# Output products as Strassen's seven half-size products in an attention and gated FFN kernel, with three attention banks, a ring of features and a row sum on GpSimd

## The chip, the cores and the metric

The kernel runs on one core of a Trainium2 chip. The metric is the device time in microseconds (us) of one execution. The kernel before took 346.88 us (median of three runs, 346.76 to 348.04). In later sessions its medians lay between 347.5 and 350.3 us, so each experiment is compared with runs of the kernel before that were made beside it on the same chip.

## The reference

```python
B, H, S, D = 8, 8, 576, 64                    # q, k, v: [B, H, S, D] float32, drawn as 0.1 * randn
k_p = k.reshape(B, H, S // 8, 8, D).mean(3)   # keys and values pooled by 8: 72 rows a head
v_p = v.reshape(B, H, S // 8, 8, D).mean(3)
attn = softmax(q @ k_p.T / sqrt(D)) @ v_p     # per head
x = attn.transpose(0, 2, 1, 3).reshape(4608, 512)
out = (relu(x @ w_gate) * (x @ w_val)) @ w_out     # 512 -> 1536 -> 512, float32
```

## The kernel before

The 4608 tokens go through the FFN in nine chunks of 512 tokens. While chunk c is in its gate and value products, TensorE also makes the output products of chunk c-1 and the attention of batch c+1. This is "the stage of chunk c". The attention of a stage is a list of small pieces of work, one after each unit of large matmuls.

```python
def scores(b, h):                      # one head: two banks, one exponential
    ps = ps_at.tile([P, 2, 512], F32)              # ps_at: 2 tiles of 2 banks
    for j, c0, i0, cnt in (...): nc.tensor.matmul(out=ps[:SP, j, ...], ...)
    nc.scalar.activation(out=e[:SP], in_=ps[:SP, :, :HS], func=AF.Exp, ...)
...
def values(b, t):                      # weights times pooled v -> px (piece_pool: 4 buffers)
...
def back(b, t, eng):                   # px -> x_T, most by a DMA transpose that SyncE issues
    eng.dma_start_transpose(out=dst, in_=x)
...
def q_dma(b):                          # q -> qT, one large DMA transpose, same queue
    nc.sync.dma_start_transpose(out=qT_tiles[b], in_=q16_tiles[b]...)
...
def prep(b, load_next):                # all on GpSimd, in this order
    for i in range(KJ // 2): run(pool_k(b, i, nc.gpsimd))
    if load_next: load_k(b + 1); load_q(b + 1); load_v(b + 1)      # 576 KB each
    for g in range(NG): run(pool_v(b, g, nc.gpsimd))
...
for c in range(1, n_chunks):
    units = weave_units(gv[:-1], outs)             # outs: 4 x (12 matmuls of 512 columns)
    if c + 2 < B: q_dma(c + 2); prep(c + 2, c + 3 < B)
    if c + 1 < B: others = attention(c + 1)        # [kt], [], four pairs of heads, values ...
    for i, unit in enumerate(units): unit(); run(others[i])
```

GpSimd's queue is in order. In the kernel before nothing in it waits for the FFN, so it runs ahead. SyncE's queue holds the transposes and the stores of finished blocks of 128 rows, also in order.

The softmax here doesn't subtract the row's maximum and nothing guards it: scores larger than these inputs give would overflow.

## Time and profile before

| what (one profiled run) | value |
|---|---|
| span | 346.0 us, TensorE busy for 96% |
| stage of chunk 1 | 30.48 us |
| stage of chunk 2 | 36.30 us, 1.15 of it waiting for features |
| stages of chunks 3 to 6 | 35.00 us each, TensorE full |
| stage of chunk 7, without attention | 31.08 us |
| from the stage of chunk 8 to the end | 46.53 us |

A stage is cut where each chunk's first gate matmul starts. Its length is what the time is made of, since TensorE hardly waits.

These are lines of the timeline of SyncE's queue in the kernel before (start us, length us, engine, line, operation, count). The length of a row is how long SyncE was held by the instructions that issue the transfers. It is not the time until the data landed, and a row of several instructions includes the gaps between them:

```profile
112.18 8.51 SPq L324 DMA_TRANSPOSE x_T<-px  x3
...
126.23 0.60 SPq L366 DMA_DIRECT2D out_dram<-fout  x1
126.94 7.27 SPq L218 DMA_TRANSPOSE qT<-q  x1
...
148.21 8.54 SPq L324 DMA_TRANSPOSE x_T<-px  x3
...
163.26 4.47 SPq L218 DMA_TRANSPOSE qT<-q  x1
```

"The time of a transpose" below is this time of SyncE; where a landing or the packets themselves were read, the text says so. A piece of features held SyncE for 3.88, 1.22 and 1.21 us in the first of these rows and for 1.45, 1.19 and 1.19 us in the row at 148.21; the rest of a row of three is mostly waiting for the next piece. The queries of a batch take 4.5 to 7.3 us, and a single store stands ahead of them.

### The profile page before, as it was taken

What the parts mean: (1) busy time and instruction counts of PE and PEld (TensorE: products, weight loads), DVE (VectorE), ACT (ScalarE), POOL (GpSimd) and SP (SyncE); (2) the same over time, 40 slices, a digit from 0 to 9 for tenths busy, and PEclk for the clock granted to TensorE, in tenths of its full rate; (3) what the DMA queues carried; (4) which work ended last, traced back from release to release, by engine and by line L of the source; (5) the groups of instructions that cost most, each with busy time, mean ns of one, the idle gap of its engine ahead of it and who ended that gap; (6) DMA issues with size and microseconds to landing.
All of it is one profiled execution on the core that took longest, in us unless ns stands there. A gap on an engine that the chain in (4) does not pass through costs nothing.

```text
span 346.0 us, 5538 instructions
## 1 busy us (share of the span) xinstructions
PE 333.7 (96%) x2140; PEld 179.3 (52%) x2140; DVE 158.7 (46%) x291; ACT 129.4 (37%) x232; POOL 132.4 (38%) x184
## 2 busy tenths in 40 slices
PE   7799999999999989999999999999999999999995
PEld 2578895455454435544545455445544444444443
DVE  7446636435624434353435343534253322398840
ACT  1344472374263225423442345234523232322221
POOL 8447509999999898307910710000000000000000
PEclk9979999999999999999999999999999999999999
DMA  7999996998996799962414351421134111211113
GB/s 114 196 205 199 167 213 116 197 167 161 142 175 112 132 165 154 190 112 60 94 40 48 78 97 34 75 53 32 30 70 52 40 32 34 57 28 35 30 58 95
DMA packets 48762, 35.36 MB, mean 102 GB/s; under 512 B 29600, under 2 KB 42144, under 8 KB 48736
## 3 DMA queue, kind: packets, MB, share of 16 engines
q0 software_dynamic: 16496, 18.88, 33.4%
q1 hardware_dynamic: 32096, 16.00, 25.0%
q8 instruction: 17, 0.28, 0.4%
q10 hardware_dynamic: 144, 0.13, 0.1%
q14 instruction: 9, 0.07, 0.1%
HBM read 37.75 MB, written 9.44 MB: 136 GB/s over the span
## 4 chain that ended last, share of the span: by engine, by line
PE 87%; DMA 6%; DVE 4%; issue 1%; POOL 1%; ACT 1%; DVEq 0%; ACTq 0%; POOLq 0%
PE mm_ps L343 51%; PE mm_ps L388 24%; PE at_ps L232 4%; DMA x_T<-px 4%; PE at_ps L302 3%; DMA v_in<-in_v_dram 2%; DVE h L359 2%; PE mm_ps L328 1%; PE mm_ps L253 1%; PE mm_ps L411 1%; PE mm_ps L178 1%; PE mm_ps L281 0%; PE mm_ps L208 0%; POOL k_in L116 0%; DVE px L312 0%
## 5 line engine op out<-in xcount | busy, mean ns | idle before, releaser
L359 DVE TENSOR_TENSOR h<-mm_ps,relu 128x512 f16<-128x512 f32 (+1 forms) x120 | 97.1, 819 | 150.3 <-PE mm_ps L343 140.1
L343 PE MATMUL mm_ps<-x_T,wg_sb 128*128 128x512 f16 (+1 forms) x480 | 113.7, 359 | 2.3 <-DMA x_T<-px 1.1
L343 PE MATMUL mm_ps<-x_T,wv_sb 128*128 128x512 f16 (+1 forms) x480 | 113.4, 359 | 0.4 <-DVE kpT1u L191 0.4
L349 ACT ACTIVATE relu<-mm_ps 128x512 f16<-128x512 f32 (+1 forms) x120 | 66.4, 553 | 118.9 <-PE mm_ps L343 115.2
L388 PE MATMUL mm_ps<-wo_sb,h 128*128 128x512 f16 x420 | 101.5, 379 | 0.4 <-DVE h L359 0.2
L343 PEld LDWEIGHTS <-wv_sb 128*128 128x128 f16 x480 | 47.1, 98 | 47.3 <-DVE kpT1u L191 0.7
L343 PEld LDWEIGHTS <-wg_sb 128*128 128x128 f16 x480 | 45.0, 99 | 38.8 <-DMA x_T<-px 1.6
L388 PEld LDWEIGHTS <-h 128*128 128x128 f16 x420 | 40.0, 98 | 45.6 <-DVE h L359 0.7
L237 ACT ACTIVATE expT<-at_ps 72x576 f16<-72x576 f32 x56 | 33.6, 642 | 19.8 <-PE at_ps L232 19.8
L397 ACT COPY fout<-mm_ps 128x512 f32<-128x512 f32 x31 | 18.1, 585 | 46.4 <-PE mm_ps L388 46.4
L145 POOL TENSOR_TENSOR tree_b<-tree_a 72x256 f32<-72x256 f32 (+1 forms) x45 | 32.5, 721 | 3.5
L312 DVE TENSOR_TENSOR px<-at_ps,prd 128x256 f16<-128x256 f32 (+1 forms) x80 | 30.2, 418 | 1.4
L139 POOL TENSOR_TENSOR tree_a<-k_in 96x512 f32<-96x512 f16 x21 | 24.1, 1149 | 15.5 <-DMA k_in<-in_k_dram 15.5
L139 POOL TENSOR_TENSOR tree_a<-v_in 72x512 f32<-72x512 f16 x24 | 27.6, 1152 | 0.1
L150 POOL TENSOR_TENSOR stat<-tree_b 72x128 f16<-72x128 f32 x24 | 10.8, 451 | 37.4 <-PE at_ps L302 35.7
L302 PEld LDWEIGHTS <-expT 72*128 72x128 f16 (+1 forms) x280 | 12.9, 100 | 8.8 <-issue 3.0
L302 PE MATMUL at_ps<-stat,expT 72*128 72x65 f16 (+1 forms) x280 | 14.7, 194 | 0.4 <-DVE stat L265 0.4
L309 DVE RECIPROCAL prd<-at_ps 128x8 f32<-128x8 f32 (+1 forms) x40 | 8.0, 201 | 13.8 <-PE at_ps L302 13.8
L330 ACT COPY x_T<-mm_ps 128x512 f16<-128x512 f16 (+1 forms) x10 | 5.6, 564 | 14.1 <-PE mm_ps L328 14.0
L150 POOL TENSOR_TENSOR kp<-tree_b 96x128 f16<-96x128 f32 x21 | 9.5, 452 | 1.6
L172 PE MATMUL mm_ps<-warm_sb 128*128 128x512 f16 x24 | 8.6, 491 | 1.2 <-DVE warm_sb L483 1.2
L232 PE MATMUL at_ps<-qT,kpT1u 128*72 128x32 f16 x64 | 9.3, 229 | 0.0
(61 smaller groups left out, 157.8 us busy)
## 6 DMA issues: line engine op xcount, KB each, us to landing
out_dram<-fout SPq DMA_DIRECT2D x31, 256.0 KB
k_in<-in_k_dram POOLq DMA_DIRECT2D x7, 576.0 KB, 7.3
q<-in_q_dram POOLq DMA_DIRECT2D x7, 576.0 KB, 9.8
v_in<-in_v_dram POOLq DMA_DIRECT2D x7, 576.0 KB, 15.1
wg_sb<-in_moe_w_gate_dram POOLq DMA_DIRECT2D x6, 256.0 KB, 11.2
wv_sb<-in_moe_w_val_dram POOLq DMA_DIRECT2D x6, 256.0 KB, 11.0
wo_sb<-in_moe_w_out_dram POOLq DMA_DIRECT2D x3, 512.0 KB, 10.3
out_dram<-fout SPq DMA_DIRECT2D x16, 64.0 KB
```

Source lines behind the costliest of these rows:

```text
L139: eng.tensor_tensor(out=cell["a"][:n], in0=src[:, :, :4 * D], in1=src[:, :, 4 * D:], op=ALU.add)
L145: eng.tensor_tensor(out=cell["c"][:n], in0=a[:n, :, :2 * D], in1=a[:n, :, 2 * D:], op=ALU.add)
L150: eng.tensor_tensor(out=out_ap, in0=c[:n, :, :D], in1=c[:n, :, D:], op=ALU.add)
L232: nc.tensor.matmul(out=ps[:SP, j, c0:c0 + cnt * QP], lhsT=kpTs[b % 2][j][:, h, :], rhs=queries(b, h, i0, cnt), start=True, stop=True,)
L237: nc.scalar.activation(out=e[:SP], in_=ps[:SP, :, :HS], func=AF.Exp, scale=EXP_SCALE)
L302: nc.tensor.matmul(out=ps[:n, half, c0:c0 + D + 1], lhsT=weights(b, h, t), rhs=stats[b % 2][:SP, g, s0:s0 + D + 1], start=True, stop=True,)
L312: nc.vector.tensor_tensor(out=x[:n, half * NG // 2:(half + 1) * NG // 2, :, :], in0=xs, in1=rd[:n, half].unsqueeze(3).to_broadcast([n, NG ...
L343: nc.tensor.matmul(out=t[:, :n], lhsT=w[:, ci, fsl], rhs=x_T[:, ci, p0:p0 + n], start=(ci == 0), stop=(ci == n_co - 1),)
L349: nc.scalar.activation(out=relu[:, :n], in_=ps[0][:, :n], func=AF.Relu)
L359: nc.vector.tensor_tensor(out=h, in0=val, in1=relu, op=ALU.mult)
L388: nc.tensor.matmul(out=t, lhsT=h_tiles[c, fo][:, ts * P:(ts + 1) * P], rhs=wo_sb[:, fo, :], start=(fo == 0), stop=(fo == n_fo - 1),)
L397: nc.scalar.copy(o, t)
```

## The change

The intent is to save arithmetic. The output product of a chunk (512 x 1536 by 1536 x 512) is cut into halves in all three directions, and Strassen's scheme needs seven half-size products in place of eight. VectorE makes the sums of h in float16 and the sums of results in float32. The rest of the change makes room for this and rearranges the start: one accumulator bank is taken from the attention, features are kept for four batches only (a ring), and k and v of batches 0 and 1 are loaded in wider rows. The core of the diff:

```diff
-    ps_at = ... bufs=2 (tiles of two banks)
+    ps_at = ... bufs=3 (tiles of one bank)
+    ps_acc = ... bufs=1
-    x_T = const_pool.tile([P, n_co, NTOK], F16, name="x_T")
+    RING = 4 * S
+    x_T = const_pool.tile([P, n_co, RING], F16, name="x_T")
-    fout_pool ... bufs=3
+    fout_pool ... bufs=2
@@ scores @@
-        nc.scalar.activation(out=e[:SP], in_=ps[:SP, :, :HS], func=AF.Exp, scale=EXP_SCALE)
+        for j, parts in ...:                       # one bank and one exponential a half
+            ps = ps_at.tile([P, 512], F32, name="at_ps", tag="at_ps")
+            ...
+            nc.scalar.activation(out=e[:SP, j, :], in_=ps[:SP, :HS], func=AF.Exp, ...)
@@ out_products, new @@
+        def pr1(): nc.scalar.copy(p1, product(a, e, True))
+        def pr2(): nc.scalar.copy(rows[0][:, :, :HD], product(b, g, False))
+        ...
+        def pr5():
+            nc.scalar.copy(p5, product(S[0], T[0], True))
+            plus(rows[1][:, :, HD:], u3, p5, nc.gpsimd)     # the only FFN work on GpSimd
+            send(1)                                         # two blocks of rows at once
+        def pr3():
+            plus(rows[0][:, :, HD:], product(S[3], h, False), u2)
+            send(0)
@@ attention @@
+        soon = 3 if b == 3 else 1                  # values of batch 3 in three units in a row
@@ main @@
+        weight_sums(nc.vector)                     # before stage 1: four sums of w_out's quarters
... (wide loads, pooling by selection matmuls, permuted h cut to 128 columns: left out)
```

## The prediction

> **What bounds the kernel now.** I read the head of the page first, then the chain that ended last, then a table of one row per chunk's stage (cut where each chunk's first gate matmul starts), and last the timeline inside a stage.
>
> ```profile
> PE 333.7 (96%) x2140; PEld 179.3 (52%) x2140; DVE 158.7 (46%) x291; ACT 129.4 (37%) x232; POOL 132.4 (38%) x184
> ...
> PE 87%; DMA 6%; DVE 4%; issue 1%; POOL 1%; ACT 1%; DVEq 0%; ACTq 0%; POOLq 0%
> ```
>
> TensorE (PE) is busy for 96% of the span and makes up 87% of the chain; no other engine reaches half. The chain also gives the price of a matmul where nothing waits (start us, length us, what):
>
> ```profile
> 276.36 3.45 PE mm_ps L343 x16
> ...
> 339.23 2.63 PE mm_ps L411 x24
> ```
>
> Sixteen 512-column matmuls in 3.45 us are 0.216 us each; twenty-four 256-column ones in 2.63 us are 0.110 us each, although each has its own weight load. Half-width products therefore cost nearly half.
>
> The stages of chunks 1 to 8 (columns: window and its length, then busy us and count of PE, weight loads, DVE, ACT, POOL; clock; DMA share; GB/s):
>
> ```profile
> 61.68:92.16 30.48, 30.48 (x203) 16.01 (x203) 14.74 (x30) 13.49 (x23) 28.59 (x40) 1.00 0.96 165
> 92.16:128.46 36.30, 35.15 (x216) 17.61 (x215) 15.02 (x30) 13.92 (x24) 33.09 (x44) 1.00 0.89 145
> 128.46:163.46 35.00, 35.00 (x215) 17.68 (x216) 13.63 (x28) 13.92 (x24) 16.83 (x23) 1.00 0.77 133
> 163.46:198.45 34.99, 34.99 (x216) 17.68 (x215) 14.33 (x29) 13.91 (x24) 15.85 (x22) 1.00 0.38 65
> ...
> 268.43:299.51 31.08, 31.08 (x145) 14.11 (x144) 8.30 (x12) 9.50 (x16) 0.00 (x0) 1.00 0.15 36
> 299.51:333.66 34.15, 33.78 (x157) 15.05 (x155) 29.53 (x13) 9.51 (x16) 0.00 (x0) 1.00 0.14 34
> ```
>
> Stage 7, which has no attention, is 144 matmuls x 0.216 = 31.1 us: nothing but its arithmetic. An attention stage adds 3.7 us of small matmuls and is again full: 35.0 of 35.0. So what a stage loses or gains in PE time or in PE waits goes straight into the span. Only stage 2 waits, 36.30 against 35.15: the chain has 12.26 us of the DMA that writes the features of batch 3 there, and PE waited for it at 127 us. Stage 8 waits a little, with DVE nearly full (29.53), because its twelve permuted products h take 2.4 us each.
>
> **What the Trainium skill says.** (1) "TensorE: Matmul & The Clock Gate", section "Back-to-back issue gap", gives N / 2.4 + 2.5 ns for a warm matmul, 216 ns at 512 and 109 ns at 256; the trace agrees (0.216 and 0.110). (2) "PSUM — Partial Sum Buffer", section "Specifications (TRN2)": eight banks of 512 float32 per partition. Before, four single-bank product tiles plus two two-bank attention tiles fill them; after, it is four, three single-bank attention tiles and one accumulator. (3) "VectorE: DVE Perf Modes", section "The perf-mode tier table": a tensor_tensor with 16-bit operands in SBUF runs at two elements a cycle, with a PSUM operand at one. No such all-16-bit operation is in this trace; the PSUM ones agree with one: 0.69 us for 512 elements and 0.42 for 256, so 1.04 ns an element and some 0.16 us fixed. (4) "SBUF — State Buffer", section "Who interferes with whom": a DVE instruction with two SBUF inputs and a GpSimd one that reads SBUF exclude each other for a whole instruction. The trace has no such meeting yet. The h products, with one SBUF input, took 0.69 us with GpSimd busy (71 us) and idle (300 us), which does not contradict it.
>
> **Gains, part by part.**
> Strassen: per chunk 48 x 0.216 = 10.37 us become 7 products x 12 matmuls x 0.110 = 9.24 us. That is 1.13 us, and for seven chunks 7.9 us, all on the path.
> Batch 3's values move to three units in a row in stage 2, so their features are sent earlier: the 1.3 us (36.30 - 35.00) goes.
> Start and chunk 0: pooling v on PE takes 10 matmuls in place of 16 for each of two batches, 12 x 0.11 = 1.3 us; the waits of 0.42 and 0.46 us just before stage 1 go, since the last feature copies move behind the next chunk's products; the key turns become 18 small matmuls in place of 7, about 0.3 us worse. Together 1.9 us. That v itself lands sooner than its 13 us I do not expect: it is the same bytes with shorter runs.
> Last stage: only 128 of 512 columns are still permuted, so h falls from 2.4 us to about 1.2 and PE's waits of 0.4 us vanish; I take 0.5 us.
> Sum of the gains: 11.6 us.
>
> **Losses, part by part.** The order of instructions of the changed kernel shows in every pair of heads that the fourth score tile waits for ACT: four one-bank tiles go through three banks. This is how the pair runs today:
>
> ```profile
> 68.45 0.29 PE L232 MATMUL at_ps<-qT,kpT0l 128*72 128x288 f16 x1
> ...
> 68.84 0.31 PE L232 MATMUL at_ps<-qT,kpT0u 128*72 128x32 f16 x2
> ...
> 68.92 1.18 ACT L237 ACTIVATE expT<-at_ps 72x576 f16<-72x576 f32 x2 [1.83 <-PE at_ps L232]
> 68.99 1.03 PE L343 MATMUL mm_ps<-x_T,wg_sb 128*128 128x512 f16 x4
> ```
>
> PE is through in 0.54 us and ACT works behind it. After, with the pair's start as zero: the first tile's data are there at 0.29, its exponential (288 of 576 columns; 0.64 us less 288 x 0.84 ns, the slope between 512 columns at 0.59 and 576 at 0.64, so 0.40) ends at 0.72, and with some 0.06 us for the semaphore the fourth tile starts at 0.78 where it would start at 0.39. That is 0.39 us of idle PE a pair. The pair that directly follows the second product is worse: ACT first copies that product (0.585 us), so its first exponential ends near 1.1 and the wait is 0.77 us. Stage 1: 4 x 0.39 = 1.6 us. Stages 2 to 6: 3 x 0.39 + 0.77 = 1.94 us each, 9.7 us. Together 11.3 us: more than Strassen gives.
>
> Weight sums: four DVE operations of 1536 elements stand before the first h of stage 1. At two elements a cycle 0.16 + 768 x 1.04 ns = 0.96 us each, 3.8 us. They start about 1.5 us after PE begins that stage's first products, and PE runs on until the key transposes need the bank that first h frees: by my count it stops for 2.4 us, and for up to 5 if GpSimd, busy there with v, holds the shared port.
>
> Sums of h: eight of 768 elements a chunk, 0.16 + 384 x 1.04 ns = 0.56 us each, 4.5 us on a DVE that has 20 us free in a stage. They lie beside PE, except that the key copies (2 x 0.75) stand behind the first two sums and the first pair needs them. If GpSimd is at work then, a sum waits up to 1.15 us, and the first pair loses up to 1 us; that can be so in stages 2 to 5, since the sum of rows on GpSimd now holds back the pooling behind it. 0 to 4 us, I take 2.
> Chunk 4 wraps round the ring: 256-column halves, 12 x 16 x 0.110 against 12 x 8 x 0.216, 0.4 us.
> Sum of the losses: 14.1 us without contention, 20.7 with all of it.
>
> **Rivals.** (a) Strassen pays: the pair's wait is no wait because PE or ACT timing slips elsewhere. Then 346.9 - 11.6 + 2.8 = about 338. For it speaks that units and warm-up matmuls were placed with care; against it, that the stages have no slack and the wait is in the order of instructions. (b) PSUM waits cancel it, without port contention: 346.9 - 11.6 + 14.1 = 349.4. (c) The same plus contention between DVE's sums and GpSimd: up to 346.9 - 11.6 + 20.7 = 356. (d) DVE becomes the bound: before it is busy 14 to 15 us of 35, and 4.5 us of sums, 2.8 us of product evictions (4 x 0.69) and some halves' fixed costs make some 24; not on average.
>
> **The range.** I put most weight on (b), some on (c), and hold a little back because the start may gain more than I can see and because the layout looks tuned: 350 us. The range is 341 to 356. Faster by over 2% (under 339.9) needs (a) whole: 0.10. Slower by over 2% (over 353.8) needs most of (c): 0.22. The rest 0.68.
>
> **What would show it.** In the stage table, stages 7 and 8 should be shorter (near 30.0 and 33), while stages 3 to 6 should be 35.5 to 36.5 although their matmuls need only 33.9. In the list of waits the second-half score tile must wait for ACT's exponential, 24 times, near 0.4 us; without those lines the main step is wrong. The sums must take 0.56 us; longer ones in stages 2 to 5 alone are the port. Stage 1 should grow from 30.5 to 34 or more, with PE idle behind the weight sums. If stages 3 to 6 are near 34, rival (a) holds.

## More of the kernel before

The timeline of GpSimd shows when the loads of batches 6 and 7 are issued:

```profile
115.99 0.54 POOL L116 DMA_DIRECT2D k_in<-in_k_dram  x1
...
136.25 0.55 POOL L116 DMA_DIRECT2D k_in<-in_k_dram  x1
```

The view of DMA issues says for the first of them (last columns: KB, us from issue to landing):

```profile
k_in<-in_k_dram POOLq DMA_DIRECT2D x1, 576.0 KB, 7.3
q<-in_q_dram POOLq DMA_DIRECT2D x1, 576.0 KB, 9.8
v_in<-in_v_dram POOLq DMA_DIRECT2D x1, 576.0 KB, 15.1
```

## The result, and the profile after

The changed kernel is correct and took 369.79 us (median of four runs: fast ones of 366.14, 369.55 and 370.03 us, and a slow one of 373.04 us), against 347.46 us for the kernel before beside it. The ratio of the fast runs is 1.0615 (95% interval 1.0511 to 1.0719), so it is slower, and outside the predicted range of 341 to 356. Ratios here are the mean time of one kernel's fast runs over that of the other's in the same rounds, so not quite the ratio of the medians.

The head of the page after and its chain (shares of the span):

```profile
PE 330.1 (91%) x2502; PEld 210.9 (58%) x2502; DVE 211.1 (58%) x437; ACT 129.9 (36%) x281; POOL 149.2 (41%) x189
...
PE 74%; DMA 14%; DVE 4%; ACT 3%; issue 2%; POOL 2%; SPq 0%; DVEq 0%; ACTq 0%; POOLq 0%
```

TensorE's work did shrink, from 333.7 to 330.1 us, but the chain's share of DMA grew from 6% to 14%. The table of stages says where (columns as in the prediction: window and its length; busy us and count of PE, weight loads, DVE, ACT, POOL; clock, DMA share, GB/s):

```profile
58.62:92.73 34.11, 31.50 (x207) 16.20 (x207) 21.34 (x40) 14.71 (x32) 32.28 (x41) 1.00 0.89 154
92.73:128.45 35.72, 34.63 (x253) 21.12 (x252) 23.16 (x46) 14.10 (x31) 23.32 (x29) 1.00 0.56 106
128.45:176.53 48.08, 35.59 (x252) 21.26 (x251) 25.09 (x46) 14.06 (x31) 24.67 (x32) 0.89 1.20 81
176.53:215.60 39.07, 36.27 (x349) 31.14 (x348) 23.09 (x46) 14.13 (x31) 16.61 (x20) 0.96 0.70 107
...
251.85:287.56 35.71, 34.44 (x252) 21.15 (x251) 21.34 (x46) 14.02 (x31) 1.27 (x1) 1.00 0.14 34
287.56:317.45 29.89, 29.89 (x181) 17.61 (x180) 14.81 (x24) 8.82 (x15) 1.27 (x1) 1.00 0.24 49
```

The stages of chunks 5 to 7 are as predicted. Chunk 3's took 13.1 us more than before (48.08 against 35.00) and chunk 4's 4.1 us more (39.07 against 34.99). In chunk 3's stage the DMA share rose to 1.20 (0.77 before), while only 81 GB/s were moved (133 before). SyncE's queue in that stage:

```profile
128.65 0.65 SPq L443 DMA_DIRECT2D out_dram<-rows  x1
129.41 16.97 SPq L288 DMA_TRANSPOSE qT<-q  x1
146.48 24.72 SPq L396 DMA_TRANSPOSE x_T<-px  x4
```

The transpose of the queries takes 16.97 us in place of 7.27. The four pieces of features behind it held SyncE for 7.32, 6.90, 7.49 and 2.73 us, where the pieces of this stage in the kernel before took 1.2 to 1.5. The last store ahead of it is the seventh, 1 MB in all, that SyncE issued from 124.11 us on. GpSimd's timeline and the landing times of the loads:

```profile
122.82 1.26 POOL L523 TENSOR_TENSOR rows<-mid,mid 128x512 f32<-128x512 f32 x1 [11.11 <-ACT mid L545]
...
131.35 0.55 POOL L124 DMA_DIRECT2D k_in<-in_k_dram  x1
```

```profile
k_in<-in_k_dram POOLq DMA_DIRECT2D x1, 576.0 KB, 36.3
q<-in_q_dram POOLq DMA_DIRECT2D x1, 576.0 KB, 38.2
v_in<-in_v_dram POOLq DMA_DIRECT2D x1, 576.0 KB, 41.6
```

In brackets stands how long the engine sat idle and for whom. GpSimd now waited 11.11 us for the fifth product's copy before its row sum, so the loads of batch 6 were issued at 131.35 us, 1.9 us into the transpose of the queries, in place of 115.99 us. They took 36 to 42 us to land in place of 7 to 15. How this reached TensorE shows in the timeline of VectorE and TensorE:

```profile
173.27 0.42 DVE L383 TENSOR_TENSOR px<-at_ps,prd 64x256 f16<-64x256 f32 x1 [15.46 <-DMA x_T<-px]
...
174.15 0.67 DVE L436 TENSOR_TENSOR h<-mm_ps,relu 128x512 f16<-128x512 f32 x1
...
174.88 1.86 PE L418 MATMUL mm_ps<-x_T,wv_sb 128*128 128x512 f16 x4 [11.42 <-DVE h L436]
```

The fifth piece of features found its buffer (one of four) still being transposed. The chain of work that ended last gives the time from the issue of the piece in that buffer to its landing (start us, length us, what):

```profile
146.48 26.70 DMA x_T<-px
```

VectorE's queue is in order, so the products h stood behind it, the banks of TensorE were not emptied, and TensorE stopped for 11.42 us. Its granted clock fell meanwhile, to 0.50 between 168 and 178 us and 0.89 on average in this stage, so the stage of chunk 4 began at half clock.

The predicted wait of the fourth score tile is there as well. This pair answers to the one that the prediction shows:

```profile
67.48 0.29 PE L304 MATMUL at_ps<-qT,kpT0l 128*72 128x288 f16 x1
67.60 0.31 PE L304 MATMUL at_ps<-qT,kpT0u 128*72 128x32 f16 x2
67.75 0.29 PE L304 MATMUL at_ps<-qT,kpT0l 128*72 128x288 f16 x1
68.26 0.30 PE L304 MATMUL at_ps<-qT,kpT0u 128*72 128x32 f16 x2 [0.23 <-ACT expT L308]
```

From the third to the fourth tile it takes 0.51 us in place of 0.12, so the wait costs 0.39 us, as predicted.

### The profile page after: what moved, and what is told of

Read it like the earlier page. It is cut to its first block, busy times and chain, and to the rows that moved or that the text cites. A ratio compares the mean times of both kernels' runs of the same rounds, so it can differ in the third digit from the quotient of the medians.

```text
span 364.4 us, 6470 instructions
## 1 busy us (share of the span) xinstructions
PE 330.1 (91%) x2502; PEld 210.9 (58%) x2502; DVE 211.1 (58%) x437; ACT 129.9 (36%) x281; POOL 149.2 (41%) x189
## 4 chain that ended last, share of the span: by engine, by line
PE 74%; DMA 14%; DVE 4%; ACT 3%; issue 2%; POOL 2%; SPq 0%; DVEq 0%; ACTq 0%; POOLq 0%
PE mm_ps L418 45%; PE acc_ps L515 15%; DMA x_T<-px 7%; PE mm_ps L465 5%; DMA out_dram<-rows 4%; PE at_ps L304 3%; DMA q<-in_q_dram 3%; PE at_ps L377 2%; ACT expT L308 2%; DVE h L436 1%; ACT rows L533 1%; PE mm_ps L565 1%; DVE px L383 1%; PE mm_ps L400 1%; DVE sum L506 1%
## 5 line engine op out<-in xcount | busy, mean ns | idle before, releaser
L418 PE MATMUL mm_ps<-x_T,wv_sb 128*128 128x512 f16 (+1 forms) x528 | 114.4, 343 | 13.1 <-DVE h L436 13.1
L436 DVE TENSOR_TENSOR h<-mm_ps,relu 128x512 f16<-128x512 f32 (+2 forms) x120 | 76.7, 639 | 85.0 <-PE mm_ps L418 77.4
L383 DVE TENSOR_TENSOR px<-at_ps,prd 128x256 f16<-128x256 f32 (+1 forms) x80 | 33.8, 423 | 18.2 <-DMA x_T<-px 15.5
L308 ACT ACTIVATE expT<-at_ps 72x288 f16<-72x288 f32 x112 | 37.2, 405 | 14.0 <-PE at_ps L304 14.0
L515 PEld LDWEIGHTS <-sum 128*128 128x128 f16 x336 | 32.6, 98 | 7.1
L515 PE MATMUL acc_ps<-wo_sums,sum 128*128 128x256 f16 x252 | 30.9, 272 | 0.0
L515 PEld LDWEIGHTS <-h 128*128 128x128 f16 x252 | 24.0, 98 | 3.9
L515 PE MATMUL acc_ps<-wo_sb,h 128*128 128x256 f16 x168 | 20.6, 273 | 0.0
L506 DVE TENSOR_TENSOR sum<-h 128x768 f16<-128x768 f16 x28 | 20.3, 764 | 0.0
L465 PE MATMUL mm_ps<-wo_sb,h 128*128 128x512 f16 x84 | 19.6, 379 | 0.0
L382 DVE RECIPROCAL prd<-at_ps 128x4 f32<-128x4 f32 (+1 forms) x80 | 13.7, 172 | 3.7 <-PE at_ps L377 3.7
L523 DVE TENSOR_TENSOR mid<-acc_ps,mid 128x512 f32<-128x512 f32 x14 | 9.6, 688 | 8.3 <-PE acc_ps L515 8.2
## 6 DMA issues: line engine op xcount, KB each, us to landing
v_in<-in_v_dram POOLq DMA_DIRECT2D x6, 576.0 KB, 16.5
wg_sb<-in_moe_w_gate_dram POOLq DMA_DIRECT2D x6, 256.0 KB, 12.1
```

Source lines behind the costliest of these rows:

```text
L308: nc.scalar.activation(out=e[:SP, j, :], in_=ps[:SP, :HS], func=AF.Exp, scale=EXP_SCALE)
L383: nc.vector.tensor_tensor(out=x[:n, half * NG // 2:(half + 1) * NG // 2, :, :], in0=pv.rearrange("p g (x c) -> p g x c", x=2)[:, :, :, :D] ...
L418: nc.tensor.matmul(out=t[:, lo:hi], lhsT=w[:, ci, fsl], rhs=x_T[:, ci, x0:x0 + hi - lo], start=(ci == 0), stop=(ci == n_co - 1),)
L436: nc.vector.tensor_tensor(out=h, in0=val, in1=relu, op=ALU.mult)
L465: nc.tensor.matmul(out=t, lhsT=h_tiles[c][:, fo, ts * P:(ts + 1) * P], rhs=wo_sb[:, fo, :], start=(fo == 0), stop=(fo == n_fo - 1),)
L506: nc.vector.tensor_tensor(out=S[k][:, i], in0=x[:, i], in1=y[:, i], op=op)
```

## The experiments

At first I held that the delay of the loads was at fault (theory L), against the banks and weight sums (B) and the stores (S). The theories changed as runs came in, and each expectation names the one of its time.

**The row sum back on VectorE.**

```diff
-            plus(rows[1][:, :, HD:], u3, p5, nc.gpsimd)
+            plus(rows[1][:, :, HD:], u3, p5)
```

> The changed kernel with one edit: the fourth sum of rows (the one of the fifth product) runs on VectorE in place of GpSimd, so GpSimd's queue has nothing in it that waits for a late product and the loads of batches 6 and 7 go out as early as in the kernel before. Theory L (late loads meet the transposes): the stage of chunk 3 falls from 48.1 us to 36 to 37, that of chunk 4 from 39.1 to 36 to 37, the transpose of the queries of batch 5 from 17 us to under 8, and the median from 369.8 to 352 to 356 us. Rival B (waits for attention banks and weight sums make up the loss, the transposes are only a symptom): under 2 us of gain, 367 us or more. Rival S (the stores of two blocks of rows at once slow the transposes, not the loads): no gain either.

Measured: runs of 353.39, 353.91, 362.34 and 364.17 us; the fast ones are 1.0131 times the kernel before. In the profile (span 352.1) the stages of chunks 3 and 4 took 36.82 and 36.16 us and the transpose of batch 5's queries 8.91 us. So moving the one instruction off GpSimd takes back most of the loss (the ratio falls from 1.0615 to 1.0131). Why two of the runs were 9 us longer is not settled, since no profile fell on one.

**Late loads in the kernel before.** GpSimd copies one column of the chunk's eleventh h and so waits for it, before the pooling and the loads.

```diff
+            if c >= 2:
+                nc.gpsimd.tensor_copy(out=gate_sb, in_=h_tiles[c, n_fo - 2][:, :1])
             gv[-1]()
```

> The kernel before with one addition: at the end of each stage from chunk 2 on GpSimd copies one column of that chunk's eleventh h, so the pooling and the loads behind it wait as they do in the changed kernel; everything else is as before. Theory L: the loads of batch 6 go out near 129 us and those of batch 7 near 170 us instead of 116 and 136, the transposes beside them take 12 us and more, the stages of chunks 3 and 4 grow by 5 us or more together, and the median is 352 us or more. Rival B or S: the loads go out late too, but the time stays within 1.5 us of 347.5.

Measured: 344.34 us, 0.9872 of the kernel before (0.9841 to 0.9902). It was 1.3% shorter, where theory L expected 352 us or more, and theory L fell. The loads were as late as expected, yet nothing crawled, that is, no transfer took several times as long as usual:

```profile
124.72 4.48 SPq L218 DMA_TRANSPOSE qT<-q  x1
144.66 8.54 SPq L324 DMA_TRANSPOSE x_T<-px  x3
```

The loads went out at 130.37 us, just after SyncE was done with this transpose at 129.20 us. So the lateness alone does no harm in this kernel. The stage of chunk 2 also lost its wait for features (34.99 us in place of 36.30).

**Loads ahead of the row sum.** The pooling of k and the loads of the batch after were put ahead of the row sum.

```diff
+        if b >= 3 and load_next:
+            for i in range(KJ // 2): run(pool_k(b + 1, i, nc.gpsimd))
+            if b + 2 < B: load_k(b + 2); load_q(b + 2); load_v(b + 2)
```

> The changed kernel with GpSimd's rows sum kept, but the pooling of k and the loads of the batch after moved ahead of it by one stage (pooling of k of batch 4 and loads of batch 5 as they were; k of batch 4 and 5 pooled, and batches 6 and 7 loaded, before the rows sum that held them back). Theory L: as without the GpSimd sum, 352 to 356 us, with the loads of batch 6 issued before 120 us. Rival: if it is GpSimd's sum itself (the shared port) and not the loads' time, no gain, 367 us or more.

Measured: 426.59 us. This run is void for its question: the pooled keys of batch 4 are written into the buffer of batch 2 in program order before batch 2's keys are read from it, so TensorE waited for GpSimd. The group of the key transposes shows it (last column: idle before, and for whom):

```profile
L248 PE MATMUL mm_ps<-ident,kp 96*128 96x96 f16 x42 | 5.4, 250 | 66.7 <-POOL kp L183 66.7
```

It passed the comparison with the reference although batch 2 must have had wrong keys, so with these inputs a correct result says little about the keys.

**The three banks alone, in the kernel before.**

```diff
-        ps = ps_at.tile([P, 2, 512], ...)          # 2 buffers
+            ps = ps_at.tile([P, 512], ...)         # 3 buffers; exponential and values in halves
```

> The kernel before with the changed kernel's attention tiles alone: three one-bank tiles in place of two two-bank ones, so each head's exponential and each piece's product are in two halves; output products, loads and features as before. My prediction's step: the pair's fourth score tile waits 0.39 us, 24 pairs, so 9 to 10 us more: 356.5 to 357.5 us. Rival: the wait is taken back by matmuls that then run later without their own waits, so under 4 us more.

Measured: 356.12 us, 1.0192 of the kernel before. That is 6.7 us by the ratio (0.0192 x 348.8), less than the 9 to 10 expected in total. Per stage it is exact: the stages of chunks 3 to 6 took 36.90 us in place of 35.00, so 1.9 us, where the prediction had said 1.94. The profiled spans differ by 8.4 us (354.4 less 346.0): 7.6 in the stages of chunks 3 to 6, 1.6 in that of chunk 1 (32.03 us), only 0.6 in that of chunk 2, which lost its wait for features here (36.90), 0.1 at the end, less 1.5 because this run starts chunk 1 at 60.17 us and not at 61.68. The pair behind an output copy shows the second size:

```profile
139.28 0.29 PE L234 MATMUL at_ps<-qT,kpT0l 128*72 128x288 f16 x1
140.16 0.30 PE L234 MATMUL at_ps<-qT,kpT0u 128*72 128x32 f16 x2 [0.59 <-ACT expT L238]
```

This is 0.88 us in place of 0.12, so 0.76 us; 0.77 had been predicted.

**Loads held until the queries are transposed.** This is the changed kernel with one column copied on GpSimd; the row sum stays there.

```diff
         if load_next:
+            nc.gpsimd.tensor_copy(out=gate_sb, in_=qT_tiles[b][:, NI - 1, :1])
             load_k(b + 1)
```

> The changed kernel with one addition: GpSimd copies one column of the transposed queries just before it issues the next batch's loads, so the loads go out only when that transpose has ended; GpSimd's rows sum stays where it is. After the run in which late loads did not hurt the kernel before, my theory is now C: what hurts is loads that are issued while the transpose of the queries runs, early or late does not matter. C expects the transpose of the queries of batch 5 near 5 to 9 us (17.0 in the changed kernel), the loads of batch 6 landing 6 to 15 us after issue (36 to 42), the stage of chunk 3 at 36 to 38 us (48.1) and the median at 352 to 357 us. If the stores of rows are what slows the transpose (theory S), it stays above 12 us and the median above 362 us.

Measured: 350.26 us beside 350.27 us of the kernel before; ratio 0.9976 (0.9908 to 1.0043). The loads of batch 6 went out even later, at 139.65 us, and landed in 6.0, 7.9 and 12.1 us. The stages of chunks 3 and 4:

```profile
128.35:164.06 35.71, 34.62 (x252) 21.10 (x251) 21.52 (x46) 14.03 (x31) 19.76 (x27) 1.00 0.74 114
164.06:200.02 35.96, 34.80 (x348) 30.48 (x347) 21.23 (x46) 14.11 (x31) 19.23 (x27) 1.00 0.61 111
```

These two stages gave back 12.4 and 3.1 us, 15.5 in all; the spans differ by 15.4 (364.4 less 349.0). By the ratios the hold is worth more, 22 us ((1.0615 - 0.9976) x 347): the profiled run of the changed kernel was its fastest. The hold moves only the loads and the pooling of v behind them, so the loss is the meeting of the loads with the transpose, whatever the reason that made them meet. The hold also shows a landing: SyncE was done with the transpose at 137.19 us, and GpSimd's copy, which waits for the data, started at 139.53.

**Loads beside the transpose in the kernel before.** As in the late-load run, on the ninth h.

```diff
+                nc.gpsimd.tensor_copy(out=gate_sb, in_=h_tiles[c, n_fo - 4][:, :1])
```

> The kernel before with the column copy of the late-load run moved up to the ninth h of the chunk, so the loads of batches 6 and 7 go out within 1 us of the start of the transpose of the queries (near 124.5 and 159.5 us). Theory C: now that they run side by side, the transposes take over 10 us, the loads over 20 us to land, and the median is 3 us or more above the late-load run's 344.3 us, though the loads are earlier. Theory S (only with the stores of whole chunks at once): transposes under 8 us and 344 to 346 us.

Measured: 344.06 us. The transpose was slowed, as theory C had it, but nothing else was:

```profile
124.51 13.05 SPq L218 DMA_TRANSPOSE qT<-q  x1
...
144.45 8.54 SPq L324 DMA_TRANSPOSE x_T<-px  x3
```

The loads had been issued at 123.64 us, ahead of it, and landed in 6.3, 11.5 and 16.5 us. The slow transpose cost no time, since the queries are needed a stage later. Side by side is therefore not enough for the pile-up.

**All mends.** The hold of the loads, the fifth product's sum on VectorE straight from the accumulator, single heads in place of pairs, weight sums in eight halves during stage 1, and three output tiles.

```diff
+            nc.gpsimd.tensor_copy(out=gate_sb, in_=qT_tiles[b][:, NI - 1, :1])
-            nc.scalar.copy(p5, product(S[0], T[0], True))
-            plus(rows[1][:, :, HD:], u3, p5, nc.gpsimd)
+            plus(rows[1][:, :, HD:], product(S[0], T[0], True), u3)
-        return [[kt], []] + pairs + [[p] for p in V[:soon]] + ...
+        return [[kt], []] + [[s] for s in Sc] + [[p] for p in V[:soon]] + ...   # soon: 2, or 3 for batch 3
-        weight_sums(nc.vector)                    # before stage 1
+                if c == 1 and i >= 5: run(w_sums[i - 5:i - 4])
-    fout_pool ... bufs=2
+    fout_pool ... bufs=3                          # half tiles in a pool of their own
```

> The changed kernel with the mends together: loads held until the transpose of the queries has ended; the fifth product's sum of rows on VectorE straight from the accumulator (no copy, no GpSimd); scores of one head per unit in place of pairs, so four tiles never stand in a row before three banks; the weight sums in eight halves among stage 1's later units; three output tiles. If all my terms are right: the stages of chunks 3 to 6 near 34.2 us, stage 1 near 30, stages 7 and 8 at 29.9, the median 336 to 340 us, faster than before by over 2%. If the collision of loads and transposes stays, a stage over 38 us and 345 us or more.

Measured: 339.25 us, 0.9667 of the kernel before (0.9602 to 0.9731). It beats both kernels. The stages of chunks 3 to 6 took 33.80, 34.04, 34.48 and 33.80 us. The stage of chunk 1, at 33.06, stayed above the 30 expected. Batch 2's pairs were left as they are there, and in the three-bank run they alone made this stage 32.03 in place of 30.48; that the weight sums, as long as 1.07 us apiece, made the rest is not shown.

**Stores behind the queries.**

```diff
-            send(1)
+            held.append(lambda: send(1))          # issued in the next stage, after q_dma
```

> The changed kernel with the stores of each chunk's rows held back to the next stage and issued behind the transpose of the queries in place of in front of it; the loads meet the transpose as in the changed kernel. Theory S (the megabyte of stores that is put into the queue at once just ahead slows the transpose): the transpose of batch 5's queries falls under 9 us, the stage of chunk 3 under 39 us, the median under 360 us. Theory C (loads and transpose alone): the transpose stays above 12 us and the median above 363 us.

Measured: 361.17 us, ratio 1.0301. The outcome fits neither column. With no stores ahead the transpose of batch 5's queries started at 124.46 us and took 2.69 us, so it was over before the loads of batch 6 went out at 133.75; those landed in 8.5 to 14.0 us beside the stores. The rest of the loss is this edit's own: ScalarE waited 4.30 us for the late stores to release the rows, in the stage of chunk 3 (40.77 us). The run moved the transpose out of the loads' way and so could not tell the theories apart.

**Queries held beside the loads, without stores.** The stores of chunks 1 and 2 were left out; the output is wrong.

```diff
+            if c > 2: send(1)                     # and send(0)
+                if i == 1 and c in (2, 3):        # holds the transpose
+                    nc.vector.tensor_copy(out=q0, in_=q0); q_dma(c + 2)
```

> The changed kernel, but the stores of rows of chunks 1 and 2 are left out (their output is wrong on purpose), and the transposes of the queries of batches 5 and 6 are held by a VectorE copy until after each stage's second gate unit, so that they start with the loads of batches 6 and 7 and not before. In the kernel before, loads and transpose side by side made the transpose 13 us and did no harm; in the changed kernel it was 17 us, the features' transposes after it took 6 us each and the loads over 36 us. Theory D (the pile-up needs the stores too: three kinds at once): here the transpose takes 13 us or less, the loads land within 17 us, the stage of chunk 3 is under 38 us, the median under 356 us. Theory C2 (in the changed kernel loads and transpose suffice): transpose over 15 us, loads over 25 us, stage of chunk 3 over 41 us, median over 360 us.

Measured: 352.78 us (1.0124 for the fast runs). The transpose came at 136.40 us, 5 us after the loads and not with them, and took 7.26 us; the loads landed in 6.1, 8.0 and 11.9 us, and chunk 3's stage took 35.71 us. That is what theory D expects, but the timing was not the one I wanted.

**Loads, queries and stores in the kernel before.** As the sixth run, with three stores of zeros ahead of the transpose.

```diff
+            if c in (3, 4, 5):
+                for i in range(3):
+                    nc.sync.dma_start(out=out[r0:r0 + P], in_=junk)
```

> The kernel before with the loads moved beside the transpose of the queries as in the earlier run (344.1 us), and three more 256 KB stores of zeros just ahead of that transpose at the start of the stages of chunks 3, 4 and 5 (to rows that are written properly at the end), so that about a megabyte of stores, the loads and the transpose are in flight together. Theory D: transpose over 15 us, loads of batch 6 over 25 us to land, the features' transposes behind them over 4 us each, and if the feature tiles run out, a stage over 38 us and a median of 348 us or more. Theory C2: as without the extra stores, transpose near 13 to 15 us, loads within 20 us, 344 to 346 us.

Measured: 345.42 us; transpose 14.00 us, loads landed in 6.3, 9.8 and 16.4 us. All three kinds in flight together did not pile up either, with the loads issued first (123.88 us, transpose at 126.42).

**Hold and single heads.** Two of the mends alone; as in the run with all mends, two pieces of values follow the heads directly, where the changed kernel had one.

```diff
+            nc.gpsimd.tensor_copy(out=gate_sb, in_=qT_tiles[b][:, NI - 1, :1])
-        return [[kt], []] + pairs + ...
+        return [[kt], []] + [[s] for s in Sc] + ...    # soon: 2, or 3 for batch 3
```

> The changed kernel with two edits: loads held until the transpose of the queries has ended (alone: 350.3 us), and from batch 3 on the scores of one head per unit in place of two, so that no fourth tile waits for an exponential. If the pair's wait costs what my prediction said (1.94 us in each of the stages 2 to 6, 9.7 us), the median is 340 to 342 us and those stages fall from about 35.8 to about 34. If the waits merely move to later matmuls: over 346 us.

Measured: 341.51 us, ratio 0.9810 (0.9757 to 0.9863): 5.8 us under the run with the hold alone by the ratios ((0.9976 - 0.9810) x 349), and 9.3 us by the profiled spans (349.0 less 339.7; the two are of different sessions). Stages of this run:

```profile
125.23:159.03 33.80, 33.80 (x252) 21.16 (x251) 21.16 (x46) 14.33 (x31) 19.56 (x28) 1.00 0.69 121
...
228.51:262.31 33.80, 33.80 (x252) 21.15 (x251) 21.13 (x46) 14.39 (x31) 1.26 (x1) 1.00 0.15 35
```

Each is full (33.80 of 33.80), 1.91 us under the 35.71 of the same stage with pairs. The waits do not move to other matmuls.

Three more runs were spent on why the transfers crawl in the changed kernel. **Queries first, no extra stores, kernel before:** the column of the tenth h.

```diff
+                nc.gpsimd.tensor_copy(out=gate_sb, in_=h_tiles[c, n_fo - 3][:, :1])
```

> The kernel before with the column copy on the tenth h, so the loads of batches 6 and 7 go out near 127 us, some 2.5 us after the transpose of the queries began (in the earlier run of this kind they went out just before it). Theory O (the order matters: loads that are issued into a transpose already under way crawl, loads issued ahead of it do not): loads land after 25 us or more, the transpose takes over 12 us. Theory D or no order: loads within 17 us, transpose 5 to 10 us, 344 to 346 us.

Measured: 344.14 us. The loads went out at 126.95 us, 2.4 us after the transpose had begun; it took 4.53 us, and they landed in 7.8, 10.4 and 15.2 us. At first I read this as "the order alone does nothing"; the table of packets below says why it does not follow.

**Queries first, no stores, changed kernel:**

```diff
+            if c > 2: send(1)                     # and send(0)
+                if c in (2, 3): nc.vector.tensor_copy(out=q0, in_=q0)
                 q_dma(c + 2)
```

> The changed kernel with the stores of rows of chunks 1 and 2 left out (wrong output on purpose) and the transposes of the queries of batches 5 and 6 held only to the start of their stage, so that the transpose begins near 130 us and the loads of batch 6 follow 1 to 2 us later, as in the changed kernel, without the stores. Theory O: loads 25 us or more to land, transpose over 12 us, stage of chunk 3 over 41 us. Theory D (stores are needed): loads within 17 us, transpose under 10 us, stage of chunk 3 under 37 us, median 351 to 355 us.

Measured: 352.30 us (1.0106), with wrong output. Without stores ahead the transpose took 2.69 us. The loads were issued 1.8 us after its start, but their first packet came at 135.72 us, when the transpose's last had begun (135.65); they landed in 7.1, 8.9 and 11.5 us, and the stage of chunk 3 took 35.71 us. VectorE's sums of h ran at that very time (133 to 144 us), so they alone are not what slows the loads.

**Queries first, with stores, kernel before:**

```diff
+                nc.gpsimd.tensor_copy(out=gate_sb, in_=h_tiles[c, n_fo - 3][:, :1])
+                nc.gpsimd.tensor_tensor(out=junk2, in0=junk2, in1=junk2, op=ALU.add)   # a delay
+            (three stores of zeros ahead of the transpose, as above)
```

> The kernel before with three extra stores of zeros ahead of the transpose of the queries (as in the run before) and the loads some 1 to 2.5 us behind the transpose's start: the order and the three kinds of transfer of the changed kernel's stage of chunk 3. Theory O together with stores: loads of batch 6 over 25 us, transpose over 15 us, and a later stage over 38 us if the feature tiles run out. If nothing happens (loads within 17 us, 344 to 347 us), the pile-up needs something else of the changed kernel, and its exact trigger stays open.

Measured: 345.77 us (runs of 344.84 to 346.22, and one of 359.83). Here the crawl appeared in the kernel before. The loads of batch 6, issued at 128.65 us, 0.9 us into the transpose:

```profile
k_in<-in_k_dram POOLq DMA_DIRECT2D x1, 576.0 KB, 21.4
q<-in_q_dram POOLq DMA_DIRECT2D x1, 576.0 KB, 25.2
v_in<-in_v_dram POOLq DMA_DIRECT2D x1, 576.0 KB, 30.6
```

The three pieces of features after them held SyncE for 6.82, 3.16 and 1.27 us, in place of 1.45, 1.19 and 1.19, and the stage grew only to 35.37 us. The expectation was met in part: k landed in 21 and not 25 us, and the queries' own transpose held SyncE for 4.50 us only, though 157 of its 2304 packets had not begun at 141.8 us, 14 us after its start. A stage later the loads followed the transpose by 0.5 us only, and there the transpose took 13.19 us while the loads landed in 8.1 to 14.4. So the crawl came where stores went ahead and the loads were issued 0.9 us (here) or 1.9 us (in the changed kernel) into the transpose.

**What the packets say.** The packed traces hold every packet with its size: 256 bytes for a transpose (2304 of them for a batch of queries), 2048 for a store, 6144 for a load of k. For the loads of batch 6 and the transpose of batch 5's queries:

| run | packets of the transpose not yet begun at the loads' first packet | loads landed in (us) |
|---|---|---|
| changed kernel | 1388 of 2304 | 36 to 42 |
| kernel before, queries first, with stores | 537 | 21 to 31 |
| kernel before, queries first, no extra stores | 125 | 8 to 15 |
| changed kernel, queries first, no stores | 0 | 7 to 12 |
| late loads; hold of the loads | 0 | 6 to 13 |
| loads ahead (sixth run, with and without stores) | 2304, all | 6 to 16 |

The crawl came in the two runs where the loads' first packet found the transpose part done (916 and 1767 packets begun). It did not come where nearly all had begun, nor where hardly any had: a stage later in the last run it was 11, and there the transpose waited and the loads did not. The two runs without stores that were to test the order did not test it, since their transposes were done or all but done. Nor were three kinds in flight: the last packet of a store had started before the first of the loads (137.52 and 138.17 us in the changed kernel, 130.40 and 132.67 in the last run), and none followed in the next 6 us. What the stores did is to draw the transpose out: with the same stores and the loads held, its packets spread over 7.3 us (131.53 to 138.80), without stores over 2.9 us. Whether loads into a half-done transpose crawl without any store before it is not tested.

## Why the prediction was wrong, point by point

**The step that failed** is "If GpSimd is at work then, a sum waits up to 1.15 us ... since the sum of rows on GpSimd now holds back the pooling behind it. 0 to 4 us, I take 2." It saw that GpSimd's queue is held back, and priced only the port that it shares with VectorE. The loads stand in the same queue behind the same sum. Held back, they met a transpose of the queries that was half done and drawn out by the stores that the change sends in bursts, and the transfers crawled. That cost 15.5 us in the profiled runs, and no term, rival or range of the prediction contained it. Rivals (a) to (d) are about banks, ports and VectorE; none asks what a changed time of issue does to the DMA queues.

**Without this the sum was right.** With the loads held, and everything else as in the change, the kernel took 350.26 us; 350.0 was predicted. Part of that is luck: beside it the kernel before took 350.27 us, so by the ratio it is 346.1 us on the scale of the prediction (0.9976 x 346.9), which is 4 us under.

**Strassen, 1.13 us a chunk:** right. The stage of chunk 7 fell from 31.08 to 29.89 us, 1.19 us, and the full stages without bank waits from 35.00 to 33.80.

**The pair's wait, 0.39 and 0.77 us, 1.94 a stage:** right. It is 0.39 and 0.76 in the timelines, 1.9 in the kernel before with three banks, and 1.91 when it is taken out of the changed kernel. It was the price of the accumulator's bank, and it was avoidable by spreading the heads over units that were free.

**Weight sums, 2.4 us:** mechanism right, size somewhat off. TensorE stood still for 1.70 us in the profile (65.33 us), and the stage of chunk 1 grew to 34.11 us, "34 or more". In other runs with the sums in the same place it took 32.25 to 37.21 us, so the meeting with GpSimd varies, as the range of up to 5 said. The four sums took 1.45 us on average in this profile and 0.95 in the run with the hold, where 0.96 had been predicted.

**Sums of h, 0.56 us:** right. They took 0.55 us on average in the stages of chunks 6 and 7, where none met an instruction of GpSimd, and 1.08 and 1.12 us in those of chunks 3 and 5, where all did (0.63 in that of chunk 8, without GpSimd and unexplained); with the hold, seven of the eight in chunk 3's stage met none and took 0.55 too. So the shared port costs. On TensorE it was two waits of 0.48 us for keys, less than the 2 us taken.

**Batch 3's values, 1.3 us:** right in effect, since chunk 2's stage no longer waits for features. The cause was only half named: in the kernel before it went away as well (34.99 us) when the loads of batch 6 were held back past the transposes at 112 to 121 us. It was gone in the three-bank run too, with loads at 115.26 us, so the loads are not shown to be the cause either.

**Start, 1.9 us:** not shown. The profiles start chunk 1 at 61.68 us before and at 58.62 after, but six variants of the kernel before, with the same start, lie at 59.24 to 60.17 (59.24, 59.29, 59.45, 59.49, 60.00, 60.17), and variants of the changed kernel at 58.42 to 60.07. A gain of 1 us or less is left, inside the spread of single runs.

**The permuted h, 0.5 us:** about 0.3. TensorE took 31.38 us before and 29.89 after from chunk 8's start to its last output products, and 1.19 of that is Strassen.

**Chunk 4's wrap round the ring, 0.4 us:** 0.25 (35.96 against 35.71 with the hold, 34.04 against 33.80 with all mends). In its reading of the stages the prediction gives the attention 3.7 us of small matmuls; its own lines give 3.9 (35.00 less 31.08), which no later sum uses.

**The end.** The prediction overlooked that two output tiles in place of three make the end wait; this answers to the end of the page:

```profile
357.41 0.59 ACT L474 COPY fout<-mm_ps 128x512 f32<-128x512 f32 x1 [4.11 <-DMA out_dram<-fout]
```

From chunk 8's start to the end it took 46.91 us after and 46.53 before, although the arithmetic shrank; with three tiles (and the other mends) it took 44.65.

**What stays open.** Why loads and a half-done transpose slow each other so much inside the DMA engines is not shown by these traces, nor whether stores are needed for it other than as a delay. That the changed kernel's crawl is the one of the last experiment is inferred from the same order and the same packets in flight; it was reproduced at 21 to 31 us, not at 36 to 42.

## What to carry to other kernels

An instruction that waits, put into an in-order queue that also issues loads, moves those loads in time: before pricing it, list what stands behind it in that queue and what else the DMA engines will be doing at the new moment. Hold large loads away from large DMA transposes by a cheap dependency if the schedule does not do it by itself, and keep bursts of stores out of the queue ahead of a transpose: here they drew it out from 2.9 to 7.3 us. Look at the packets when you ask what was in flight; the rows of the issuing queue do not tell it. When a bank is taken from a pool, look at whether the burst of tiles that needs it can be spread over units that are free; here that returned 1.9 us a stage, more than Strassen's 1.2.

## What the Trainium skill lacked or had wrong

- "DMA: Bandwidth & Descriptors", section "Rules for kernel authors", says in its row on silent corruption that a transpose next to ordinary DMAs needs nothing. That row is about the result, and no run here contradicts it. The section lacks the time: beside loads the transpose of the queries held SyncE for up to 16.97 us in place of about 4.5, and loads took 36 to 42 us to land in place of 7 to 15 when they were issued 1.9 us into it with stores ahead.
- No page that I read gives a price for loads and a transpose in flight together: in the stage of chunk 3 the DMA share was 1.20 at 81 GB/s, against 0.74 at 114 GB/s for the same stage with the loads held.
- "SBUF — State Buffer", section "Who interferes with whom", agreed with the runs: sums of h of 768 elements took 0.55 us where they met no instruction of GpSimd and up to 1.55 us beside it. No page that I read prices what holding back GpSimd's queue does through the loads issued from it; here that was worth 15.5 us.
